# Top-k attention and a PReLU MLP on one core: small values of VectorE in a PSUM bank, the hidden layer in halves, MLP steps of two blocks side by side

## The chip, the core and the metric

The kernel runs on one core of a Trainium2 chip. The metric is the device time of one execution in microseconds (us); the time of a kernel is the median of several runs. Five engines work side by side, each with its own queue in program order: TensorE (PE, with its weight loads PEld), VectorE (DVE), ScalarE (ACT), GpSimd (POOL) and SyncE (SP), which here issues all DMAs. An instruction waits at the head of its engine's queue until what it needs is there.

## The reference

```python
def _attn_ref(q, k, v):            # (8, 8, 576, 64) each
    top_k = 32
    scale = 1.0 / np.sqrt(D)
    scores = scale * np.matmul(q, k.transpose(0, 1, 3, 2))
    kth = np.partition(scores, -top_k, axis=-1)[..., -top_k:-top_k + 1]
    scores = np.where(scores >= kth, scores, -1000000000.0)
    scores = scores - np.max(scores, axis=-1, keepdims=True)
    attn = np.exp(scores)
    attn = attn / (np.sum(attn, axis=-1, keepdims=True) + 1e-09)
    return np.matmul(attn, v)

def _moe_ref(x, w_in, w_out, alpha):   # x (4608, 512), d_ff 2048
    h = x @ w_in
    g = np.maximum(h, 0.0) + alpha * np.minimum(h, 0.0)
    return g @ w_out
```

Each of 64 heads has 576 x 576 scores; of each row only the 32 largest stay. The eight heads of a batch entry side by side are x, which goes through an MLP with a PReLU of one slope per hidden unit.

## The kernel before

A batch entry is a block: 576 tokens, eight heads in four pairs. The rows of scores are cut into duos of two tiles of 128 rows x 576; a pair has four duos of both heads' 128 rows, and two pairs share a fifth for their last 64 rows. So a block has 18 duos and the program 144. The last block takes its duos in the order of the tokens rather than of the pairs.

One turn of the main loop (lines 452 to 489) is a slot. It runs ten stages, each on another duo, so that a duo passes through the engines over several slots. `Ordered` (line 21) keeps every engine's instructions in the order in which the program is written, so the order of the calls in the loop is the order of the queues.

- `st_qk(n+2)` (line 150): TensorE computes the scores of the duo two ahead into `ps_sc`, four banks of PSUM with no second buffer. `st_exit(n+1)`: ScalarE copies scores to `s_sb`.
- `st_phase1(n)` (line 174), VectorE: MAX8 over six groups of 96 columns gives 48 candidates for each row, `cand`. `top` and `bot` (lines 185 and 186) are the elementwise larger and smaller of each second group and its neighbour in reverse; from these, with `hi`, `neg` and `n8`, comes a threshold near the 32nd largest, `p9[:, :, 0]`.
- `st_count(n-1)`, ScalarE: the sign against that threshold (`sg`) with its sum, `cs`, which is the count. `st_y(n-1)`, GpSimd: `y` = scores times `sg`.
- `st_phase2(n-2)` (line 216), VectorE: the eight largest of `y`; `eq` compares the constants `io9` with the count, `pk` picks with it from `p9`, a sum gives `KT`, the exact threshold.
- `st_relu(n-2)` (ScalarE), `st_sub(n-2)` (GpSimd) and `st_exp(n-3)` (ScalarE) mask the scores and take exp; SP's DMA transposes the weights to `wT`.
- `st_av(n-5)`: TensorE multiplies with v, with a column of ones for the sum (`xo`, or `xm` for the shared duo). `st_norm(n-5)` (line 271), VectorE: reciprocal `rz` and product, into `x`. `st_xT` (line 288): when a pair is through, SP's DMA transposes `x` into `xT`; with the fourth pair of a block, `mlp_ready` (line 311) queues the MLP of the block.
- `prep(n, 4)` (line 432): when a pair comes up in four slots, TensorE transposes its k and q (`tps`), ScalarE copies kT and VectorE qT.

The MLP of a block is a list of units (lines 309 to 361). Sixteen units compute 128 hidden rows each for all 576 tokens: eight matmuls into `ph`, in two halves of 288 columns in two banks, and one relu over both, in turn by VectorE and ScalarE (`relu`, line 365). The PReLU is split: w_out scaled by 1 - alpha takes the relu, and a product `w_lin_b` = w_in diag(alpha) w_out, computed once, takes x itself. Then each of five token tiles has two units that add both products into `pz`, 20 matmuls of 512 columns, and an output copy `o_sb`. At the end of each slot `owed` grows by 2.2 (4.0 in the last slots, up to 6.0) and units run while it is positive; a unit costs 1.0 to 2.6. There is one list, so a block's second product follows its first.

PSUM has eight banks: four for `ps_sc`, two for `ps_h` (`ph` and the transposes `tps`, one buffer of two banks), one for `pz`, one for `xo`.

The first slots also load the weights: two units a slot of `wt_units` (line 373), w_in first, then w_out, whose copies ScalarE scales.

If a threshold could not be found, a flag starts the general path behind the fast one; here it does not run.

Of the kernel before, what the change touches and what calls it, by code (L numbers as in the profile page):

```python
# [12 lines left out]
ALU = mybir.AluOpType  # L13
# [22 lines left out]
def fast_path(tc, q, k, v, moe_w_in, moe_w_out, moe_alpha, out, flag):  # L36
# [32 lines left out]
    with ExitStack() as ctx:  # L69
# [4 lines left out]
        qk_p = pool("qk", 5)  # L74
        s_p = pool("s", 6)
# [3 lines left out]
        xp = pool("xp", 2)  # L79
        ps_s = pool("ps_s", 1, space=PSUM)  # L80
        ps_h = pool("ps_h", 1, space=PSUM)
# [5 lines left out]
        io9 = const.tile([128, 9], FP32, name="io9")  # L87
# [10 lines left out]
        xs = [const.tile([128, 5, 128], BF16, name=f"x_{i}") for i in range(5)]  # L98
# [26 lines left out]
        def transpose_one(p, which, eng):  # L125
            t = st.pop((which, p))
            ps = ps_h.tile([128, 2, 512], FP32, name="tps", tag="h")
            for c in range(4):
                PE.transpose(ps[:, 0, 128 * c:128 * c + 128], t[:, c, :], ident_f)
            PE.transpose(ps[:, 1, 0:64], t[0:64, 4, :], ident_f[0:64, 0:64])  # L130
            dst = qk_p.tile([128, S], FP32, name=f"{which}T", tag=f"{which}T")
            if eng is ACT:
                ACT.copy(dst[:, 0:512], ps[:, 0, :])
                ACT.copy(dst[:, 512:S], ps[:, 1, 0:64])
            else:
                DVE.tensor_copy(dst[:, 0:512], ps[:, 0, :])
                DVE.tensor_copy(dst[:, 512:S], ps[:, 1, 0:64])
            (qT if which == "q" else kT)[p] = dst
# [35 lines left out]
        def st_phase1(n):  # L174
            s = T["s", n]
            c = two.tile([128, 2, NG, 8], FP32, name="cand", tag="cand")
# [7 lines left out]
            top = two.tile([128, 2, NG // 2, 8], FP32, name="top", tag="top")  # L184
# [3 lines left out]
            hi = two.tile([128, 2, 8], FP32, name="hi", tag="hi")  # L188
            for i in range(2):
                DVE.max(out=hi[:, i, :], in_=bot[:, i, :, :])  # L190
            DVE.tensor_scalar(neg[:, :, 0:24], top.rearrange("p a b c -> p a (b c)"), -1.0, None, ALU.mult)
            DVE.tensor_scalar(neg[:, :, 24:31], hi[:, :, 0:7], -1.0, None, ALU.mult)
            n8 = two.tile([128, 2, 8], FP32, name="n8", tag="n8")
# [6 lines left out]
        def st_count(n):  # L200
            s, p9 = T["s", n], T["p9", n]
            sg = two.tile([128, 2, S], BF16, name="sg", tag="sg")
# [13 lines left out]
        def st_phase2(n):  # L216
# [3 lines left out]
            eq = two.tile([128, 2, 9], FP32, name="eq", tag="eq")  # L220
# [6 lines left out]
        def st_relu(n):  # L227
            s = T["s", n]
            r = two.tile([128, 2, S], BF16, name="r", tag="r")
# [41 lines left out]
        def st_norm(n):  # L271
# [5 lines left out]
            if d[0] == "n":  # L277
                _, p, j = d
                DVE.tensor_tensor(xs[p % 5][:, j, :].rearrange("p (h d) -> p h d", h=2), xo[:, :, 0:64],
                                  rz[:, 0:2].unsqueeze(2).to_broadcast([128, 2, 64]), ALU.mult)  # L280
            else:
                for i in range(2):
                    DVE.tensor_tensor(xs[d[1 + i] % 5][0:64, 4, :].rearrange("p (h d) -> p h d", h=2),
# [4 lines left out]
        def st_xT(n):  # L288
# [3 lines left out]
            for p in ps_:  # L292
# [7 lines left out]
                if b < B - 1:  # L300
                    SP.dma_start_transpose(t, xs[p % 5].rearrange("p a b -> p (a b)"))
                else:
                    SP.dma_start_transpose(t[:, j:j + 1, :], xs[p % 5][:, j, :])
# [5 lines left out]
        units = []  # L309

        def mlp_ready(b, j):
# [6 lines left out]
            gt = gp.tile([128, NFT, ntok], BF16, name="gT", tag="gT")  # L318
            if ntok == S:
                def unit(f):  # L320
                    ph = ps_h.tile([128, 2, 512], FP32, name="ph", tag="h")
                    for hh in range(2):
                        for kk in range(4):
                            PE.matmul(ph[:, hh, 0:288], w_in_b[kk][:, 128 * f:128 * f + 128],
# [127 lines left out]
        for n in range(ND + 9):  # L452
# [9 lines left out]
            if on(n - 1):  # L462
                st_y(n - 1)
# [316 lines left out]
```

## Time and profile before

| | us |
|---|---|
| median of 3 runs | 1562.38 |
| lowest and highest | 1562.21, 1563.31 |
| profiled execution | 1564.27 |
| its span in the profile | 1562.4 |
| VectorE busy | 1204.5 (77%) |
| TensorE busy | 976.3 (62%) |
| ScalarE busy | 835.7 (53%) |
| GpSimd busy | 765.1 (49%) |
| mean granted TensorE clock | 0.69 of full |

The profile names buffers without their numbers, so `p` is p9, `n` is n8, `io` is io9 and `x` and `w` are the tiles of x and of the attention weights. A busy TensorE is not TensorE at its peak. All helper calls have line 31, so rows are told apart by tiles. The number in square brackets at the end of a row of the time order is the idle time ahead of it and what ended it.

### The profile page before, as it was taken

To read this page: it belongs to the slowest core of one execution; us is meant where nothing else is said; L and a number is where in the kernel's file an instruction comes from. 1 tells how busy PE (TensorE), PEld (TensorE's weight loads), DVE (VectorE), ACT (ScalarE), POOL (GpSimd) and SP (SyncE) were. 2 spreads that over 40 slices of the span, in tenths; PEclk is the share of its full clock that TensorE was granted. 3 is DMA by queue.
4 is the path that set the end of the run, shared out by engine and by line. 5 is a ranking of instruction groups with operands and counts; after the bars stand their busy time and mean duration, and the time that the engine had idled before them with its cause. 6 is when DMAs were issued, how large, how long until landed. Compare 5 with 4: busy or idle time off the path is not lost.

```text
span 1562.4 us, 18744 instructions
## 1 busy us (share of the span) xinstructions
PE 976.3 (62%) x5248; PEld 533.3 (34%) x5282; DVE 1204.5 (77%) x4191; ACT 835.7 (53%) x1360; POOL 765.1 (49%) x676
## 2 busy tenths in 40 slices
PE   4432365776567774777657675567647746468776
PEld 2221133443234332443334333343324423234444
DVE  5985545799948998599957999499976975948891
ACT  3564644566626665366635666266644654535561
POOL 4653443466525655256625666156643553514550
PEclk9755575578655885568756886578855777657878
DMA  3534422234321343124312343214331243202222
GB/s 89 120 101 101 102 46 57 49 64 94 69 37 40 84 79 68 41 45 101 70 37 48 79 88 60 48 34 86 76 65 41 57 91 72 46 18 45 61 53 49
DMA packets 346000, 102.00 MB, mean 65 GB/s; under 512 B 337168, under 2 KB 337184, under 8 KB 345888
## 3 DMA queue, kind: packets, MB, share of 16 engines
q1 hardware_dynamic: 345888, 100.73, 30.4%
q8 instruction: 44, 0.72, 0.2%
q14 instruction: 68, 0.56, 0.1%
HBM read 36.71 MB, written 9.44 MB: 30 GB/s over the span
## 4 chain that ended last, share of the span: by engine, by line
DVE 62%; PE 19%; ACT 8%; DMA 4%; issue 3%; SPq 2%; POOL 1%; ACTq 0%; POOLq 0%; DVEq 0%
DVE cand L31 14%; DVE p L31 12%; PE ph L31 11%; DVE bot L31 8%; DVE pk L31 6%; PE ps_sc L31 4%; DVE neg L31 3%; DVE top L31 3%; DVE eq L31 3%; ACT sg L31 3%; DVE gT L31 3%; SPq L31 2%; DVE n L31 2%; DVE x L31 2%; PE tps L31 2%
## 5 line engine op out<-in xcount | busy, mean ns | idle before, releaser
L31 POOL TENSOR_TENSOR y<-s_sb,sg 128x576 f32<-128x576 f32 x288 | 362.2, 1279 | 620.2 <-ACT sg L31 620.2
L31 PE MATMUL ps_sc<-kT,qT 64*128 64x64 f32 (+3 forms) x1280 | 308.7, 624 | 241.6 <-ACT s_sb L31 240.5
L31 POOL TENSOR_TENSOR s_sb<-s_sb,r 128x576 f32<-128x576 f32 x288 | 363.5, 1283 | 119.9 <-ACT r L31 119.6
L31 PE MATMUL ph<-xT,w_in_b 128*128 128x288 bf16 (+2 forms) x1216 | 240.6, 367 | 132.0 <-DMA xT<-x 45.9
L31 ACT ACTIVATE sg<-s_sb,p 128x576 bf16<-128x576 f32 x288 | 220.3, 767 | 138.2 <-DVE rz L31 130.7
L31 DVE MAX8 cand<-s_sb 128x8 f32<-128x96 f32 x1728 | 288.9, 244 | 3.5 <-ACT s_sb L31 3.5
L31 PEld LDWEIGHTS ps_sc<-kT,qT 64*128 64x128 f32 (+1 forms) x1280 | 147.3, 253 | 394.8 <-ACT s_sb L31 254.5
L31 ACT ACTIVATE r<-s_sb,KT 128x576 bf16<-128x576 f32 x288 | 207.5, 768 | 115.4 <-DVE KT L31 113.3
L31 DVE MAX8 p<-y 128x8 f32<-128x576 f32 x288 | 204.0, 747 | 31.3 <-POOL y L31 31.3
L31 PEld LDWEIGHTS <-w_in_b 128*128 128x128 bf16 x1216 | 138.4, 129 | 220.6 <-issue 145.5
L31 DVE TENSOR_SCALAR gT<-ph 128x576 bf16<-128x576 f32 (+2 forms) x66 | 48.7, 738 | 181.9 <-PE ph L31 181.9
L31 ACT ACTIVATE gT<-ph 128x576 bf16<-128x576 f32 (+2 forms) x66 | 41.9, 635 | 273.3 <-PE ph L31 273.1
L31 PEld LDWEIGHTS <-wT 128*128 128x128 bf16 (+3 forms) x1600 | 109.0, 112 | 214.0 <-issue 146.9
L31 PE MATMUL xo<-v,wT 128*128 128x65 bf16 (+1 forms) x1280 | 114.6, 214 | 102.4 <-DVE x L31 78.6
L31 ACT ACTIVATE w<-s_sb 128x1152 bf16<-128x1152 f32 x144 | 165.4, 1149 | 0.0
L31 PE MATMUL pz<-w_out_b,gT 128*128 128x512 bf16 (+1 forms) x638 | 165.0, 406 | 0.2 <-issue 0.2
L31 ACT COPY s_sb<-ps_sc 128x1152 f32<-128x1152 f32 x144 | 158.2, 1098 | 7.4 <-PE ps_sc L31 7.4
L31 DVE TENSOR_TENSOR bot<-cand 128x48 f32<-128x48 f32 x144 | 159.8, 1109 | 0.0
L31 DVE SCALAR_TENSOR_TENSOR pk<-eq,p 128x18 f32<-128x18 f32 x144 | 108.9, 756 | 5.0
L31 PEld LDWEIGHTS <-gT 128*128 128x128 bf16 (+1 forms) x640 | 66.9, 109 | 83.5 <-issue 26.9
L31 DVE TENSOR_TENSOR top<-cand 128x48 f32<-128x48 f32 x144 | 70.8, 492 | 4.9
L31 DVE COPY qT<-tps 128x512 f32<-128x512 f32 x64 | 26.1, 449 | 62.1 <-PE tps L31 62.1
(48 smaller groups left out, 799.4 us busy)
## 6 DMA issues: line engine op xcount, KB each, us to landing
k_st<-in_k_dram SPq DMA_DIRECT2D x64, 128.0 KB, 2.6
q_st<-in_q_dram SPq DMA_DIRECT2D x64, 128.0 KB, 2.5
v_st<-in_v_dram SPq DMA_DIRECT2D x64, 128.0 KB, 2.4
out_dram<-o_sb SPq DMA_DIRECT2D x32, 256.0 KB, 2.5
w_st<-in_moe_w_in_dram SPq DMA_DIRECT2D x16, 256.0 KB, 3.5
w_st<-in_moe_w_out_dram SPq DMA_DIRECT2D x16, 256.0 KB, 3.3
wT<-w SPq DMA_TRANSPOSE x144, 3.4
k_st<-in_k_dram SPq DMA_DIRECT2D x64, 16.0 KB, 2.2
```

The lines of the kernel that those rows point to most:

```text
L31: return self.tc.keep_in_program_order(f(*a, **kw))
```

## The change

- A PSUM bank of its own, `small` (pool `ps_d`), holds values that VectorE alone uses: the constants `io9`, every second group of candidates (`lo`), `top`, `hi`, `n8` and `eq`, in two places that duos take in turn. The other groups of candidates (`up`), `bot`, `neg`, `p9` and `pk` stay in SBUF. `bot` is computed ahead of `top`.
- That bank comes from `ps_h`, which has one now. `ph` is one half of 288 columns, a step is four matmuls and a relu of 288; 32 steps make a block. The transposes of k and q go through the one bank in two pieces, 512 columns and the 64-column tail (`tpt`), each with its copy.
- The MLP has two lists, `fq` for the first product and `oq` for the second, whose units are quarters of a token tile: one matmul with `w_lin_b` and four with `w_out_b`. A block's second product is queued when its first is through, and the next block's first product may run beside it. At a block's first step all second-product units of the block two before are run.
- In a slot there are three places for a first-product step and two for a second-product one, fed by allowances of 1.9 and 1.2 a slot (at most 6.0 and 4.0), and of 4.5 and 2.5 from slot 130 on, with three more of each at the end of such slots. `st_xT` moves behind the scores of the slot.
- Buffers: qT and kT 4 each instead of 5, `s_sb` 5 instead of 6, `x` 4 instead of 5, `xT` 3 instead of 2; `sg` and `r` share three where they had two each. `gT` of the last block has its own tag. The loop is one turn shorter.

```diff
-        qk_p = pool("qk", 5)
-        s_p = pool("s", 6)
+        qk_p = pool("qk", 4)
+        s_p = pool("s", 5)
...
+        small = ps_d.tile([128, 512], FP32, name="small")
+        io9 = small[:, 500:509]
...
-            ps = ps_h.tile([128, 2, 512], FP32, name="tps", tag="h")
+            ps = ps_h.tile([128, 512], FP32, name="tps", tag="h")
             for c in range(4):
...
+            copy(dst[:, 0:512], ps)
+            ps = ps_h.tile([128, 64], FP32, name="tpt", tag="h")
+            PE.transpose(ps, t[0:64, 4, :], ident_f[0:64, 0:64])
+            copy(dst[:, 512:S], ps)
...
-                    DVE.max(out=c[:, i, g, :], in_=s[:, i, GW * g:GW * g + GW])
-            up, lo = c[:, :, 0::2, :], c[:, :, 1::2, ::-1]
+                    DVE.max(out=(lo if g % 2 else up)[:, i, g // 2, :], in_=s[:, i, GW * g:GW * g + GW])
...
-            DVE.tensor_tensor(top, up, lo, ALU.max)
-            DVE.tensor_tensor(bot, up, lo, ALU.min)
+            DVE.tensor_tensor(bot, up, lo[:, :, :, ::-1], ALU.min)
+            DVE.tensor_tensor(top, up, lo[:, :, :, ::-1], ALU.max)
...
-            eq = two.tile([128, 2, 9], FP32, name="eq", tag="eq")
+            eq = small[:, 240 * (n % 2) + 128:240 * (n % 2) + 146].rearrange("p (i c) -> p i c", i=2)
...
+            r = two.tile([128, 2, S], BF16, name="r", tag="sg", bufs=3)
...
+            def unit(i):
+                if i == 0:
+
+                    while oq and oq[0][0] <= me - 2:
+                        oq.pop(0)[1]()
...
+                    f, t0 = i // 2, 288 * (i % 2)
+                    for kk in range(4):
+                        PE.matmul(ph, w_in_b[kk][:, 128 * f:128 * f + 128],
+                                  flat[kk][:, t0:t0 + 288], start=(kk == 0), stop=(kk == 3))
+                    relu(gt[:, f, t0:t0 + 288], ph)
...
+                PE.matmul(z[0:m, :], flat[a][:, t0:t0 + m], w_lin_b[a], start=(a == 0), stop=False)
+                for f in range(4 * a, 4 * a + 4):
...
-        for n in range(ND + 9):
+        for n in range(ND + 8):
...
+            end = n >= ND - 14
+            fo = min(fo + (4.5 if end else 1.9), 6.0)
+            oo = min(oo + (2.5 if end else 1.2), 4.0)
...
                 st_y(n - 1)
+            f_unit()
             if on(n):
                 st_phase1(n)
...
                 st_norm(n - 5)
-                st_xT(n - 5)
+            f_unit()
+            o_unit()
             if on(n + 2):
                 st_qk(n + 2)
+            f_unit()
+            o_unit()
+            if on(n - 5):
+                st_xT(n - 5)
             prep(n, 4)
...
+            if end:
+                for _ in range(3):
+                    f_unit()
+                    o_unit()
```

Three places show how the order of the engines changes. The first is VectorE in phase 1, with the waits on semaphores in brackets (DVE_49 is VectorE's own). Before, from the last candidates to the threshold p:

```order
L31 MAX cand<-s_sb 128x8 x11
L31 TENSOR_TENSOR top<-cand 128x48 [waits DVE_49]
L31 TENSOR_TENSOR bot<-cand 128x48
L31 MAX hi<-bot 128x8 [waits DVE_49]
L31 MAX hi<-bot 128x8
L31 TENSOR_SCALAR neg<-top 128x2x24
L31 TENSOR_SCALAR neg<-hi 128x2x7 [waits DVE_49]
L31 MAX n_10947<-neg 128x8 [waits DVE_49]
L31 MAX n_10947<-neg 128x8
L31 TENSOR_SCALAR p_10950<-n_10947 128x2 [waits DVE_49]
```

After, `small` standing for lo, top, hi and n8:

```order
L31 MAX small<-s_sb 128x8 [waits DVE_49]
L31 TENSOR_TENSOR bot<-up,small 128x48 [waits DVE_49]
L31 TENSOR_TENSOR small<-up,small 128x48
L31 MAX small<-bot 128x8 [waits DVE_49] x2
L31 TENSOR_SCALAR neg<-small 128x2x24 [waits DVE_49]
L31 TENSOR_SCALAR neg<-small 128x2x7
L31 MAX small<-neg 128x8 [waits DVE_49] x2
L31 TENSOR_SCALAR p_7165<-small 128x2 [waits DVE_49]
```

The same instructions, with bot ahead of top, and with more of them waiting for VectorE's own semaphore; five of the six MAX into `small` ahead of bot have such a wait too.

The second is VectorE where a block ends, from the product of the shared duo (xm) to the candidates of the next slot. Before:

```order
L31 TENSOR_TENSOR x_132<-xm,rz 64x128
L31 TENSOR_TENSOR x_133<-xm,rz 64x128
L31 TENSOR_SCALAR gT<-ph 128x576 x3
L31 MAX p_5521<-y 128x8 x2
L31 TENSOR_TENSOR eq<-io_103,cs 128x18
L31 SCALAR_TENSOR_TENSOR pk<-eq,p_5521 128x18
L31 TENSOR_REDUCE KT<-pk 128x2
L31 MAX cand<-s_sb 128x8 x12
```

After:

```order
L31 TENSOR_TENSOR x_137<-xm,rz 64x128
L31 TENSOR_TENSOR x_138<-xm,rz 64x128
L31 MAX p_6993<-y 128x8 x2
L31 TENSOR_TENSOR small<-small,cs 128x18
L31 SCALAR_TENSOR_TENSOR pk<-small,p_6993 128x18
L31 TENSOR_REDUCE KT<-pk 128x2
L31 TENSOR_SCALAR gT<-ph 128x288
L31 MAX up<-s_sb 128x8
```

Three relus of 576 columns stood behind x; now one of 288 stands between KT and the candidates.

The third is TensorE where a pair's k and q are transposed, from the end of the attention product. Before:

```order
L31 MATMUL xo<-v_3_117,wT 128x65
L31 MATMUL ps_sc<-kT,qT 128x512 x2
L31 MATMUL ps_sc<-kT,qT 128x64 x2
L31 MATMUL tps<-ident_f,k_st 128x128 x4
L31 MATMUL tps<-ident_f,k_st 128x64
L31 MATMUL tps<-ident_f,q_st 128x128 x4
L31 MATMUL tps<-ident_f,q_st 128x64
```

After, from the last matmul of a quarter of the second product (pz) that stands behind a half of ph:

```order
L31 MATMUL pz<-w_out_b_150,gT 128x512
L31 MATMUL ps_sc<-kT,qT 128x512 x2
L31 MATMUL ps_sc<-kT,qT 128x64 x2
L31 MATMUL tps<-ident_f,k_st 128x128 x4
L31 MATMUL tpt<-ident_f,k_st 128x64
L31 MATMUL tps<-ident_f,q_st 128x128 x4
L31 MATMUL tpt<-ident_f,q_st 128x64
```

MLP steps now stand between the attention product and the scores, and each tail is a tile of its own in the one bank.

## Rows read from the trace of the kernel before

**Rows 1.** The page, part 1: busy time, share of the span and instructions.
```profile
PE 976.3 (62%) x5248; PEld 533.3 (34%) x5282; DVE 1204.5 (77%) x4191; ACT 835.7 (53%) x1360; POOL 765.1 (49%) x676
```

**Rows 2.** Windows: length; busy (instructions) PE, PEld, DVE, ACT, POOL; PEclk, DMA, GB/s.
```profile
838.80:974.30 135.50, 89.50 (x504) 47.68 (x505) 131.33 (x459) 88.19 (x143) 83.83 (x72) 0.76 0.35 70
797.20:838.80 41.60, 26.89 (x116) 15.07 (x117) 16.58 (x51) 10.73 (x19) 7.55 (x6) 0.52 0.22 46
1344.00:1523.00 179.00, 122.05 (x733) 71.03 (x735) 143.69 (x471) 93.09 (x150) 82.99 (x66) 0.68 0.21 44
1523.00:1562.30 39.30, 27.25 (x269) 17.48 (x269) 5.87 (x18) 7.83 (x12) 2.52 (x2) 0.89 0.22 50
```

**Rows 3.** VectorE in order of time, one slot: start us, length us, operation.
```profile
709.41 0.17 DVE L31 TENSOR_REDUCE KT<-pk 128x2 f32<-128x18 f32 x1
709.50 2.01 DVE L31 MAX8 cand<-s_sb 128x8 f32<-128x96 f32 x12
711.54 0.33 DVE L31 TENSOR_TENSOR top<-cand 128x48 f32<-128x48 f32 x1
711.80 1.31 DVE L31 TENSOR_TENSOR bot<-cand 128x48 f32<-128x48 f32 x1
...
715.79 0.70 DVE L31 TENSOR_TENSOR eq<-io,cs 128x18 f32<-128x18 f32 x1
716.53 1.20 DVE L31 SCALAR_TENSOR_TENSOR pk<-eq,p 128x18 f32<-128x18 f32 x1
717.76 0.17 DVE L31 TENSOR_REDUCE KT<-pk 128x2 f32<-128x18 f32 x1
```

**Rows 4.** Instructions by tile: ns shortest/median/longest, first and last start us, shapes.
```profile
L31 DVE TENSOR_TENSOR bot<-cand x144: 193/1309/1319, 14.9 to 1511.0; 128x48 f32<-128x48 f32 x144
L31 DVE SCALAR_TENSOR_TENSOR pk<-eq,p x144: 177/1177/1208, 29.1 to 1521.5; 128x18 f32<-128x18 f32 x144
L31 DVE TENSOR_TENSOR x<-xo,rz x128: 290/291/293, 60.8 to 1527.0; 128x128 bf16<-128x128 f32 x128
L31 DVE RECIPROCAL rz<-xo x128: 155/163/172, 60.6 to 1526.7; 128x2 f32<-128x2 f32 x128
L31 POOL TENSOR_TENSOR s_sb<-s_sb,r x288: 1268/1279/1340, 31.4 to 1525.1; 128x576 f32<-128x576 f32 x144
```

**Rows 5.** VectorE and TensorE in order of time, at the start of two blocks.
```profile
623.19 0.76 DVE L31 TENSOR_SCALAR gT<-ph 128x576 bf16<-128x576 f32 x1 [5.16 <-PE ph L31]
...
802.61 1.36 PE L31 MATMUL ph<-xT,w_in_b 128*128 128x288 bf16 x5 [0.93 <-DMA xT<-x]
...
804.01 0.76 DVE L31 TENSOR_SCALAR gT<-ph 128x576 bf16<-128x576 f32 x1 [5.17 <-PE ph L31]
```

**Rows 6.** TensorE and VectorE in order of time, where a pair is transposed.
```profile
867.73 1.41 PE L31 MATMUL tps<-ident_f,q_st 128*128 128x128 f32 x5 [1.66 <-ACT kT L31]
...
869.45 0.81 DVE L31 COPY qT<-tps 128x512 f32<-128x512 f32 x2
```

**Rows 7.** TensorE in order of time: scores, attention product and pz at both clock levels.
```profile
854.93 2.40 PE L31 MATMUL ps_sc<-kT,qT 64*128 64x512 f32 x8 [1.48 <-ACT s_sb L31]
...
863.50 1.30 PE L31 MATMUL ps_sc<-kT,qT 64*128 64x512 f32 x8 [1.46 <-ACT s_sb L31]
...
884.61 0.81 PE L31 MATMUL pz<-w_lin_b,xT 128*128 128x512 bf16 x3 [0.16 <-issue]
...
887.08 0.78 PE L31 MATMUL xo<-v,wT 128*128 128x65 bf16 x10
...
900.39 1.49 PE L31 MATMUL pz<-w_lin_b,xT 128*128 128x512 bf16 x3 [0.34 <-issue]
```

**Rows 8.** VectorE in order of time: the KT reductions that end two stages.
```profile
232.36 0.17 DVE L31 TENSOR_REDUCE KT<-pk 128x2 f32<-128x18 f32 x1
...
1343.95 0.17 DVE L31 TENSOR_REDUCE KT<-pk 128x2 f32<-128x18 f32 x1
```

**Rows 9.** Waits of ScalarE from 110 to 235 us: total us, times, longest us.
```profile
ACT w_out_b L31 <- DMA w_st<-in_moe_w_out_dram: 45.7, 11, 7.5
```

More of the change, by code (lines that the diff above doesn't have):

```diff
@@ L78, in fast_path @@
         gp = pool("gp", 2)
-        xp = pool("xp", 2)
+        xp = pool("xp", 3)
         ps_s = pool("ps_s", 1, space=PSUM)
+        ps_d = pool("ps_d", 1, space=PSUM)
         ps_h = pool("ps_h", 1, space=PSUM)
@@ L97, in fast_path @@
             POOL.memset(t[:, :, S:640], 0.0)
-        xs = [const.tile([128, 5, 128], BF16, name=f"x_{i}") for i in range(5)]
+        xs = [const.tile([128, 5, 128], BF16, name=f"x_{i}") for i in range(4)]
         for t in xs:
@@ L201, in st_count @@
             s, p9 = T["s", n], T["p9", n]
-            sg = two.tile([128, 2, S], BF16, name="sg", tag="sg")
+            sg = two.tile([128, 2, S], BF16, name="sg", tag="sg", bufs=3)
             cs = three.tile([128, 2], FP32, name="cs", tag="cs", bufs=4)
@@ L342, in mlp_ready @@
[L342 to L361 removed]
+            me = len(made)
@@ new lines, in mlp_ready @@
+            made.append(0)
+            hold = {}
+            big = ntok == S
+            cw = 288 if big else 4 * ntok
+            def unit(i):
+                if i == 0:
+                    while oq and oq[0][0] <= me - 2:
+                        oq.pop(0)[1]()
+                    hold["g"] = gp.tile([128, NFT, ntok], BF16, name="gT", tag="gT" if big else "gs")
+                gt = hold["g"]
+                ph = ps_h.tile([128, cw], FP32, name="ph", tag="h")
+                if big:
+                    f, t0 = i // 2, 288 * (i % 2)
[3 more added lines that the diff above has]
+                    relu(gt[:, f, t0:t0 + 288], ph)
+                else:
+                    for e in range(4):
+                        f = 4 * i + e
+                        for kk in range(4):
+                            PE.matmul(ph[:, ntok * e:ntok * e + ntok], w_in_b[kk][:, 128 * f:128 * f + 128],
+                                      flat[kk][:, tok0:tok0 + ntok], start=(kk == 0), stop=(kk == 3))
+                    relu(gt[:, 4 * i:4 * i + 4, :].rearrange("p a t -> p (a t)"), ph)
+                if i == nu - 1:
+                    for t0 in range(tok0, tok0 + ntok, 128):
+                        for a in range(4):
+                            oq.append((me, lambda t0=t0, a=a: part(t0, a)))
@@ new lines, in mlp_ready, with part @@
+            nu = 32 if big else 4
+            for i in range(nu):
+                fq.append((me, lambda i=i: unit(i)))
+            def part(t0, a):
+                m = min(128, tok0 + ntok - t0)
+                gt = hold["g"]
+                if a == 0:
+                    hold["z"] = ps_z.tile([128, DMODEL], FP32, name="pz", tag="z")
+                z = hold["z"]
+                PE.matmul(z[0:m, :], flat[a][:, t0:t0 + m], w_lin_b[a], start=(a == 0), stop=False)
+                for f in range(4 * a, 4 * a + 4):
+                    PE.matmul(z[0:m, :], gt[:, f, t0 - tok0:t0 - tok0 + m], w_out_b[f],
+                              start=False, stop=(f == NFT - 1))
+                if a == 3:
+                    o = io.tile([128, DMODEL], FP32, name="o_sb", tag="io")
+                    ACT.copy(o[0:m, :], z[0:m, :])
+                    SP.dma_start(out[S * b + t0:S * b + t0 + m, :], o[0:m, :])
```

101 lines of the change are left out of this document (31 added, 70 removed).

## Prediction

> **What bounds the kernel now.** I read the page's busy shares first [rows 1]: VectorE is busy 77% of the 1562.4 us span and no other engine over 62%, but a share over the whole span mixes stages. The windows [rows 2] separate them. From 838.80 to 974.30, 16 slots (a slot is one turn of the main loop, from one KT reduction to the next), VectorE is busy 131.33 of 135.50 us: it sets the pace, at 8.47 us a slot, of which ScalarE needs 5.5 and GpSimd 5.2. From 797.20 to 838.80, two slots, it is busy 16.58 of 41.60: there it waits. One slot of the first kind in order of time [rows 3] is without gaps, yet three instructions on 18 to 48 numbers per partition take 0.70, 1.20 and 1.31 us.
>
> The instructions by tile [rows 4] say why. bot runs from 193 to 1319 ns and pk from 177 to 1208 at one and the same shape; seven forms do this (eq, top, the two neg and p<-n are the others), and all of them take their inputs from SBUF. Instructions with one operand in PSUM do not vary: x takes 290 to 293 ns over 128 instances, rz 155 to 172. The ceiling of the spread is one GpSimd instruction, 1279 ns in the median (the last row of the group). So these small instructions stand behind GpSimd's tensor_tensor of the moment, and a PSUM operand spares x that.
>
> **Part 1, small values to PSUM.** With eq, pk, bot and top at their shortest (0.16, 0.18, 0.19, 0.21 us), the slot of [rows 3], 8.35 us from KT to KT, becomes 8.35 - 0.54 - 1.02 - 1.12 - 0.12 = 5.55 us.
>
> Added: waits of VectorE on itself. The order shows that `small` is guarded as one thing: the second MAX into hi, the second into n8 and the first neg now wait for the instruction ahead. In [rows 3] cand, which waits for nothing on VectorE, starts 0.08 us before KT ends, and KT, which waits for pk, 0.03 us after pk ends, so a wait costs 0.11 us. Three are 0.33; neg<-hi loses one, mostly covered, and I take 0.30. The five waits between the MAX into `small` reach back over an `up` MAX, whose pitch of 0.16 us (twelve in 2.01) covers them: 0, or 5 x 0.11 = 0.55 us a slot if the `up` counts too. No row of before has VectorE write to PSUM; between a gain, which nothing excludes, and some dearer write I take zero, by rz and x, which read PSUM at no visible surcharge.
>
> [...]
>
> **Part 2, h in halves and overlapped blocks.** The work keeps its size. A block of 18 slots has 32 halves, 1.78 a slot, and 20 quarter parts of five matmuls, 1.11 a slot. Half of the relus fall to VectorE: a 576-column relu takes 0.76 us [rows 5], 288 columns then some 0.45, and 0.37 with the overlap to the next: 0.89 x 0.37 = 0.33 us a slot. The two qT copies (0.81 us together [rows 6]) come four times in 18 slots and get one more wait: 0.19. The slot becomes 5.55 + 0.30 + 0.33 + 0.19 = 6.37 us; ScalarE and GpSimd come close but stay under it. 18 slots are 114.7 us; today a block is 804.01 - 623.19 = 180.8 us [rows 5].
>
> At a block's start three relus in a row each wait 5 us for two steps of eight matmuls, and the next slot waits too. The new code spends at most three halves a slot, so this burst goes. What is late next there is the transpose of x: VectorE goes idle at 798.84 (804.01 less 5.17), and ph goes on at 802.61 [rows 5], 3.8 us later. The first half's relu now stands between phase 2 (1.8 us) and phase 1, so VectorE waits 3.8 + 0.6 + 0.1 - 1.8 = 2.7 us, once a block.
>
> The remaining edits I cost at nothing. With five s buffers the copy of slot n+1 takes the one that exp read a slot earlier on the same engine. In the ring of three for sg and r, r waits for the y of its slot before, which phase 2 has waited for anyway, and sg for a subtraction that exp has waited for. Four buffers of qT and kT hold at most three pairs until the last block, four of x those of two pairs and the next two. The transposes of x on SP now stand behind the store of an output tile, which waits for ScalarE's o_sb: up to 1 us in the 2.7, once a block, if a store falls there; wT, behind them in SP's queue, is wanted two slots later.
>
> **Where time comes back.** The q and k transposes stay behind the scores on TensorE and gain two round trips, since the 64-column tails now wait for the head's copy out of the one bank. In [rows 6] the q transposes end at 869.14 and VectorE takes up the copy at 869.45: just in time at 8.4 us a slot. VectorE will be there 2 us sooner, and the two tails add some 0.8 us. So 2.8 us of waiting, four times a block: 11.2 us. Bounds: 0 if TensorE gets to it sooner, 5 us each if a quarter part stands in front.
>
> [...] By [rows 7] a matmul of 512 columns has a pitch of 0.43 or 0.216 us (three in 1.49 and 0.81 us, less the last one's 0.634 or 0.379, over two). A slot's scores are 2.40 or 1.30, xo 0.78 or a little more, the halves 1.78 x 0.96 or 0.49, the parts 1.11 x 2.14 or 1.08, the transposes 0.22 x 2.82 or half: 7.9 us at the lower level, 4.5 at the higher. At 6.37 us the lower one does not fit in the 11 slots of a block that hold both kinds of MLP work: 11 x 1.5 = 17 us if all were slow, 0 if none. I take a third, 5.5 us, since the steady stretch, with the same round trips, has the higher level half of its time.
>
> A block is then 114.7 + 2.7 + 11.2 + 5.5 = 134.1 us.
>
> **The sum**, along the KT marks of [rows 8].
> To 232.36 us: nine slots of today, from 30 us on, are VectorE's and lose 2 us each; the others wait for weights behind SP's queue (ScalarE for w_st, 45.7 us [rows 9]) and keep their time. 232.4 - 18 = 214.4.
> 232.36 to 1343.95: 1111.6 us, six blocks of 180.8 and 26.8 us where the loads of the last block's four pairs come close together on SP; their order is the same, I keep 26. 6 x 134.1 + 26 = 830.6.
> From there to the end, 218.4 us today. VectorE is busy 143.69 of the first 179.00 us and TensorE 122.05 [rows 2]. VectorE sheds 46, but TensorE inherits the twenty parts that the sixth of the eight blocks leaves behind, 20 x 1.08 = 22 us: 144 us of TensorE, some 17 of waits, and the same tail of 39: 200.
> 214.4 + 830.6 + 200 = 1245 us of span. The profiled execution took 1564.27 us against its span of 1562.4; the median of the runs is 1562.38. With 1.9 us on top: 1247 us.
>
> **The rivals.**
> TensorE becomes the bound. Halves, parts and transposes that share one bank keep it waiting for relus, the clock stays low, and slots stay at 8.35 us: a block 18 x 8.35 + 2.7 = 153; 6 x 153 + 26 + 214 + 205 + 2 = 1365. For it: 7.9 us of slow work, and 0.52 granted where TensorE was busy 26.89 of 41.60. Against: 0.76 at the same share in the steady stretch.
> Operands in PSUM cost more than rz shows. x takes 98 ns more than the shortest bot for 80 columns more; 0.03 us each at most, 0.2 a slot, 30 us: 1277. [...]
> The contention stays, because a PSUM operand does not spare these forms. Slots are 8.65 us, and only the boundary's 28 us go: a block 180.8 - 28 + 8 = 161; 6 x 161 + 26 + 232 + 212 + 2 = 1438. Against: x and rz.
> No stall comes back, all is VectorE's: 6 x 114.7 + 26 + 212 + 185 + 2 = 1113.
> Slower: the one ps_h bank. Every half waits for the relu of the half ahead, which stands in VectorE's queue behind phase 1 or in ScalarE's behind exp; the scores, placed behind the second half, are late, and then the copy of the scores, the count and y. It decides from 10.05 - 6.37 = 3.7 us of waiting in every slot; two waits of 2.1 us make 10.6 us a slot and a block 194: 6 x 194 + 26 + 232 + 215 + 2 = 1639. Against: ScalarE has 3 us of each 8.47 to spare.
>
> **How the numbers follow.** Forecast 1247 (1150 to 1310 with its bounds) 0.54, TensorE-bound 0.17, PSUM surcharge 0.08, contention stays 0.08, no stall 0.08, slower 0.04, no effect 0.01. From 1150 to 1400 lie the first three, 0.79. A measurement of this kernel can tell about 0.2% from no change. Faster 0.95, same 0.01, slower 0.04.
>
> **What would show it.** Right: bot, pk, eq, top, neg and p<-n constant at 160 to 230 ns; 5.9 to 6.5 us from KT to KT in a plain slot; no run of ph steps at a block's start; VectorE idle before qT in four slots of 18. Wrong: a spread up to 1.3 us that stays; VectorE idle before gT in most slots, with a clock near 0.5; a pitch of 0.27 us between the MAX into `small`; a last stretch that is longer than today's.

## The result, and the profile after

The changed kernel takes 1296.82 us in the median (1288.59 to 1304.06, four runs) beside 1562.75 for the kernel before (four runs): a ratio of 0.8297, 95% interval 0.8247 to 0.8347. It is faster, as forecast, and inside the range; the point, 1247, was 50 us too low. The profiled execution took 1296.23 us, of which the span is 1294.2.

Busy time, share of the span and instructions, part 1 of the page of after (compare [rows 1]):

```profile
PE 881.2 (68%) x5282; PEld 481.4 (37%) x5282; DVE 896.7 (69%) x4247; ACT 836.6 (65%) x1416; POOL 759.8 (59%) x675
```

VectorE lost 307.8 us of busy time at a few more instructions. Over the whole span no engine stands out any more: four lie between 59 and 69%. That share mixes stages. In the six blocks, in the windows below, VectorE is busy 670.94 of 846.50 us, more than any other engine, and of the 136.0 us of a block (the mean of five) it waits 18.3.

VectorE of after by tile: ns shortest/median/longest, first and last start, shapes (compare [rows 4]):

```profile
L31 DVE TENSOR_TENSOR bot<-up,small x144: 203/204/206, 14.5 to 1229.9; 128x48 f32<-128x48 f32 x144
L31 DVE SCALAR_TENSOR_TENSOR pk<-small,p x144: 176/176/179, 28.7 to 1240.0; 128x18 f32<-128x18 f32 x144
L31 DVE TENSOR_TENSOR small<-small,cs x144: 156/165/167, 28.5 to 1239.8; 128x18 f32<-128x18 f32 x144
L31 DVE MAX8 small<-bot x288: 194/195/196, 14.9 to 1230.4; 128x8 f32<-128x24 f32 x144
```

bot, whose median was 1309 ns, is constant at 204, and pk at 176 in place of 1177. One slot of VectorE in order of time, start and length in us (compare [rows 3]):

```profile
561.13 0.17 DVE L31 TENSOR_REDUCE KT<-pk 128x2 f32<-128x18 f32 x1
561.22 0.25 DVE L31 MAX8 up<-s_sb 128x8 f32<-128x96 f32 x1
...
563.27 0.20 DVE L31 TENSOR_TENSOR bot<-up,small 128x48 f32<-128x48 f32 x1
...
565.36 0.45 DVE L31 TENSOR_SCALAR gT<-ph 128x288 bf16<-128x288 f32 x1
...
567.05 0.17 DVE L31 TENSOR_TENSOR small<-small,cs 128x18 f32<-128x18 f32 x1
567.25 0.18 DVE L31 SCALAR_TENSOR_TENSOR pk<-small,p 128x18 f32<-128x18 f32 x1
567.46 0.17 DVE L31 TENSOR_REDUCE KT<-pk 128x2 f32<-128x18 f32 x1
```

The slot is 6.33 us from KT to KT with a relu in it and 5.96 to 5.97 without; it was 8.35. The stretches of after by windows (length; busy of PE, PEld, DVE, ACT, POOL; granted clock), cut at the KT marks that answer to [rows 8]:

```profile
28.90:219.10 190.20, 85.51 (x411) 44.48 (x412) 105.78 (x508) 112.20 (x182) 98.48 (x92) 0.64 0.41 95
219.10:1065.60 846.50, 619.51 (x3727) 336.31 (x3725) 670.94 (x3184) 610.63 (x1044) 564.28 (x489) 0.82 0.41 82
1065.60:1240.20 174.60, 130.23 (x876) 72.72 (x873) 103.53 (x478) 97.48 (x165) 82.58 (x67) 0.89 0.25 53
1240.20:1294.20 54.00, 30.61 (x219) 19.34 (x219) 5.32 (x18) 6.78 (x10) 3.82 (x4) 0.63 0.15 32
```

The six blocks went from 1111.6 to 846.5 us and the start from 232.4 to 219.1; the end went from 218.4 to 228.6, so it grew by 10 us. All of the gain is in the blocks and the start.

VectorE and TensorE in order of time at a block's start and in the slot behind it, where a pair is transposed; in brackets the idle time and what ended it (compare [rows 5, 6]):

```profile
511.10 0.40 PE L31 MATMUL ph<-xT,w_in_b 128*128 128x288 bf16 x1 [4.39 <-DMA xT<-x]
...
512.87 0.46 DVE L31 TENSOR_SCALAR gT<-ph 128x288 bf16<-128x288 f32 x1 [2.67 <-PE ph L31]
...
518.77 0.65 PE L31 MATMUL tps<-ident_f,k_st 128*128 128x128 f32 x4 [0.55 <-DVE gT L31]
520.10 0.27 PE L31 MATMUL tpt<-ident_f,k_st 64*128 64x64 f32 x1 [0.68 <-ACT kT L31]
520.67 0.66 PE L31 MATMUL tps<-ident_f,q_st 128*128 128x128 f32 x4 [0.30 <-ACT kT L31]
...
521.37 0.69 DVE L31 COPY qT<-tps 128x512 f32<-128x512 f32 x1 [2.65 <-PE tps L31]
522.42 0.22 DVE L31 COPY qT<-tpt 128x64 f32<-128x64 f32 x1 [0.36 <-PE tpt L31]
```

The burst of three relus is gone. What is left are one wait for xT, behind it one or two shorter waits for the next halves (1.0 to 3.2 us a block), and, four times a block, the chain of k and q through the one bank. VectorE's largest waits over the whole span (total us, times, longest):

```profile
DVE qT L31 <- PE tps L31: 117.2, 32, 16.7
DVE gT L31 <- PE ph L31: 110.8, 44, 20.7
DVE p L31 <- POOL y L31: 44.2, 20, 7.8
```

### The profile page after: what moved, and what is told of

The parts are those of the page before. It is cut to its first block, busy times and chain, and to the rows that moved or that the text cites. A ratio compares the mean times of both kernels' runs of the same rounds, so it can differ in the third digit from the quotient of the medians.

```text
span 1294.2 us, 18779 instructions
## 1 busy us (share of the span) xinstructions
PE 881.2 (68%) x5282; PEld 481.4 (37%) x5282; DVE 896.7 (69%) x4247; ACT 836.6 (65%) x1416; POOL 759.8 (59%) x675
## 4 chain that ended last, share of the span: by engine, by line
DVE 46%; PE 24%; ACT 13%; DMA 6%; issue 4%; SPq 3%; POOL 3%; ACTq 0%; POOLq 0%
DVE small L31 15%; DVE p L31 11%; DVE up L31 6%; PE pz L31 6%; PE ph L31 6%; PE ps_sc L31 4%; PE tps L31 4%; SPq L31 3%; ACT sg L31 3%; DVE gT L31 3%; DMA w_st<-in_moe_w_out_dram 2%; ACT r L31 2%; DVE neg L31 2%; ACT s_sb L31 2%; DVE x L31 2%
## 5 line engine op out<-in xcount | busy, mean ns | idle before, releaser
L31 POOL TENSOR_TENSOR y<-s_sb,sg 128x576 f32<-128x576 f32 x288 | 361.8, 1277 | 409.6 <-ACT sg L31 409.6
L31 PE MATMUL ps_sc<-kT,qT 64*128 64x64 f32 (+3 forms) x1280 | 256.3, 533 | 102.4 <-ACT s_sb L31 102.3
L31 PE MATMUL ph<-xT,w_in_b 128*128 128x288 bf16 (+2 forms) x1216 | 212.7, 316 | 162.6 <-DVE gT L31 63.2
L31 DVE MAX8 p<-y 128x8 f32<-128x576 f32 x288 | 204.2, 747 | 44.2 <-POOL y L31 44.2
L31 ACT ACTIVATE r<-s_sb,KT 128x576 bf16<-128x576 f32 x288 | 207.2, 768 | 33.7 <-DVE KT L31 27.5
L31 PEld LDWEIGHTS ps_sc<-kT,qT 64*128 64x128 f32 (+1 forms) x1280 | 126.1, 216 | 268.9 <-issue 148.2
L31 DVE MAX8 small<-s_sb 128x8 f32<-128x96 f32 x864 | 216.7, 251 | 0.0
L31 DVE MAX8 up<-s_sb 128x8 f32<-128x96 f32 x864 | 211.1, 244 | 3.1 <-ACT s_sb L31 3.1
L31 PEld LDWEIGHTS <-w_in_b 128*128 128x128 bf16 x1216 | 114.8, 111 | 201.8 <-issue 164.9
L31 PE MATMUL pz<-w_out_b,gT 128*128 128x512 bf16 (+1 forms) x640 | 187.0, 420 | 0.0
L31 PE MATMUL xo<-v,wT 128*128 128x65 bf16 (+1 forms) x1280 | 113.1, 212 | 49.0 <-DMA wT<-w 28.2
L31 DVE TENSOR_SCALAR gT<-ph 128x288 bf16<-128x288 f32 (+2 forms) x122 | 56.7, 465 | 110.9 <-PE ph L31 110.8
L31 ACT ACTIVATE gT<-ph 128x288 bf16<-128x288 f32 (+2 forms) x122 | 50.8, 416 | 120.3 <-PE ph L31 120.3
L31 PE MATMUL pz<-w_lin_b,xT 128*128 128x512 bf16 (+1 forms) x160 | 70.6, 441 | 2.8 <-ACT o_sb L31 2.7
```

Of the source, the lines that this page charges most:

```text
L31: return self.tc.keep_in_program_order(f(*a, **kw))
```

## The experiments

The theory was that the two parts take away two separate things, the contention of small SBUF operands with GpSimd and the burst of first-product steps at a block's start, and that the transposes give some of it back. The rival was that one of the parts does all of it, or that small instructions are slow for a reason other than GpSimd. A question came with the result: where the 50 us beyond the forecast lie. Lengths of the stretches of every run, from the KT marks of its profile (us; a block is the mean of the five that hold no stall of loads):

| kernel | time | start | one block | six blocks | end |
|---|---|---|---|---|---|
| before | 1562.8 | 232.4 | 181.2 | 1111.6 | 218.4 |
| after | 1296.8 | 219.1 | 136.0 | 846.5 | 228.6 |
| e1_sbuf | 1495.2 | 233.3 | 164.3 | 1010.9 | 248.1 |
| e2_onelist | 1469.4 | 218.4 | 166.8 | 1039.4 | 207.1 |
| e3_qact | 1288.4 | 220.5 | 134.5 | 837.2 | 228.6 |
| e4_spread | 1285.9 | 219.7 | 136.8 | 850.6 | 216.6 |
| e5_tails | 1260.9 | 215.7 | 131.2 | 813.5 | 230.6 |
| e6_late | 1301.2 | 216.6 | 138.4 | 859.6 | 222.9 |
| e7_nosub | 1424.0 | 219.4 | 164.4 | 1011.9 | 191.0 |
| e8_all | 1251.5 | 214.2 | 132.4 | 822.7 | 212.1 |
| e9_split | 1308.4 | 217.0 | 137.7 | 857.5 | 229.0 |
| e10_three | 1264.9 | 216.7 | 133.2 | 828.1 | 218.1 |
| e11_even | 1254.2 | 215.6 | 133.3 | 828.5 | 203.6 |
| e12_best | 1231.3 | 214.7 | 130.4 | 809.7 | 205.5 |

**e1_sbuf: only the place of the small values undone.**

```
-        small = ps_d.tile([128, 512], FP32, name="small")
+        small = const.tile([128, 512], FP32, name="small")
```

> The changed kernel with the one tile small in SBUF instead of in its PSUM bank; order, waits and everything else as they are. Theory (a PSUM operand spares these instructions the turn of GpSimd's tensor_tensor): bot, pk, eq, top, neg and p spread again from 0.2 to 1.3 us, some 2.4 us a slot come back, plain slots are 8.3 to 8.7 us, VectorE busy near 1230 us, the time 1440 to 1560 us (part of it is absorbed by the waits for qT and gT that the changed kernel has). Rival (the order of bot and top, the own-semaphore waits and the new MLP schedule made the gain, the place does not matter): 1285 to 1310 us and constant durations.

Measured: 1495.2 us, 0.9574 of before (0.9560 to 0.9588). Same order, same waits, another memory, and the spread is back:

```profile
L31 DVE TENSOR_TENSOR bot<-up,small x144: 207/333/1280, 14.5 to 1429.5; 128x48 f32<-128x48 f32 x144
L31 DVE SCALAR_TENSOR_TENSOR pk<-small,p x144: 178/1197/1204, 29.0 to 1438.9; 128x18 f32<-128x18 f32 x144
```

So the memory in which the operands lie is the cause, not the rewriting of the chain.

**e2_onelist: the small values stay in PSUM, but the MLP steps run from one list at a slot's end, as before.**

```
-            fo = min(fo + (4.5 if end else 1.9), 6.0)
-            oo = min(oo + (2.5 if end else 1.2), 4.0)
+            owed = min(owed + (4.0 if end else 2.2), 6.0)
...
+            while (fq or oq) and owed > 0:
```

> The changed kernel with the MLP in one list as before: halves and quarter parts, each block's second product right behind its first, run at the slot's end by one allowance of 2.2 a slot (4.0 in the last 14, at most 6.0), a half at 0.5 and a part at 1.1, and the transpose of x ahead of the scores. Theory (the overlap of two blocks takes away the burst at a block's start and nothing else): plain slots stay at 6.0 to 6.3 us, each block begins with some twelve halves at 1.8 us and the wait for xT, 20 to 30 us more per block at the start; the time 1380 to 1480 us. Rival (once VectorE is fast, TensorE's sum of work sets the time whatever the order): within 20 us of 1297.

Measured: 1469.4 us, 0.9408 (0.9394 to 0.9422). Plain slots are 5.97 us, but the slots at a block's start 27.5 and 19.7 us, and VectorE waits for the first product 117 times:

```profile
DVE gT L31 <- PE ph L31: 286.2, 117, 5.7
```

With before, e1, e2 and after, the parts stand nearly in a square: the values without the schedule give 92 us, the schedule without the values 66, both 266. The square is not clean, since e1 and e2 both keep the halves, the one bank for the transposes and the other numbers of buffers. The two parts are not separate. A slot lasts as long as its slower side: with the burst left in, TensorE's steps between two relus hold up two slots and faster VectorE instructions only wait longer; with the contention left in, VectorE holds 8.2 to 8.5 us in a plain slot and the MLP steps hide behind that.

**e7_nosub: the kernel before without the masking subtraction on GpSimd** (the weights are the exponentials of all scores).

```
-                POOL.tensor_tensor(s[:, i, :], s[:, i, :], r[:, i, :], ALU.subtract)
+                pass
```

> The kernel before with one part left out: the masking subtraction on GpSimd, half of GpSimd's large instructions; the weights are then the exponentials of all scores. Theory (VectorE's small instructions stand behind the GpSimd instruction of the moment): bot, pk, eq and top keep their longest of some 1.2 to 1.3 us, but about half as often, their sum over a slot falls from 2.8 us above the shortest to 1 to 1.8 us, and the time falls to 1340 to 1460 us. Rival (they are slow for a reason of their own, in SBUF, whatever GpSimd does): the mean of bot and pk as before, 1540 to 1565 us.

Measured: 1424.0 us in a single run, inside the theory's range. The small values lie in SBUF as before, and only GpSimd does less:

```profile
L31 DVE TENSOR_TENSOR bot<-cand x144: 193/202/1320, 14.9 to 1376.3; 128x48 f32<-128x48 f32 x144
L31 DVE SCALAR_TENSOR_TENSOR pk<-eq,p x144: 177/179/1204, 29.1 to 1384.3; 128x18 f32<-128x18 f32 x144
```

The longest stay as they were, and fewer are caught: 118 of 144 bot and 82 of 144 pk last over 0.5 us before, 46 and 51 here, about half of them together, as the theory had it. The medians fall to the shortest because less than half are left; the means are 513 and 530 ns where they were 1109 and 756. The trace of the kernel before shows what they stand behind. GpSimd in the slot of [rows 3]:

```profile
710.54 2.51 POOL L31 TENSOR_TENSOR s_sb<-s_sb,r 128x576 f32<-128x576 f32 x2 [1.19 <-ACT r L31]
...
715.19 2.51 POOL L31 TENSOR_TENSOR y<-s_sb,sg 128x576 f32<-128x576 f32 x2 [2.14 <-ACT sg L31]
```

GpSimd's second instruction of each pair ends at 713.05 and 717.70 us; bot ends at 713.11 and pk at 717.73. Over the whole run the long bot and pk end 0.06 and 0.03 us, in the median, after a GpSimd instruction. So it is GpSimd's instruction of the moment that the small ones stand behind. For bot and pk that is up to 1.1 us on an instruction of 0.2.

**e3_qact: the q copies on ScalarE.**

```
-                    transpose_one(p, "q", DVE)
+                    transpose_one(p, "q", ACT)
```

> The changed kernel with the copies of the q transposes on ScalarE, as those of k, instead of on VectorE. Theory (VectorE's 131 us of waits for qT, four slots of 10 us in 18, are the chain of k transposes, copies, q transposes in one bank, and cost time because VectorE stands in that chain): those waits go, the four slots fall to 6.3 to 8 us, ScalarE takes some 25 us of copies; 1210 to 1255 us. Rival (ScalarE, with 5.5 to 6 us a slot, is the next bound: the count behind the copies is late, y is late and VectorE waits for GpSimd's y instead): 1280 to 1310 us, with VectorE's wait for y well over its 44 us.

Measured: 1288.4 us, 0.8261 (0.8232 to 0.8289). The theory missed: the 8 us below the changed kernel are inside the spread of the two kernels' runs. VectorE's waits for q are gone, but most of the same time stands elsewhere:

```profile
DVE gT L31 <- PE ph L31: 199.0, 74, 20.7
DVE p L31 <- POOL y L31: 66.4, 31, 10.3
DVE rz L31 <- PE xo L31: 50.1, 18, 12.2
```

The time is in the rival's range, and VectorE does wait longer for y, 66.4 us where it was 44.2. But more of it stands before the first product, 199.0 where it was 110.8. TensorE waits 44.0 us before the tails where it waited 47.6: the chain through the bank is about as long whoever copies, and the next half waits behind it.

**e5_tails: the 64-column tails through the bank of xo.**

```
-            ps = ps_h.tile([128, 64], FP32, name="tpt", tag="h")
+            ps = ps_x.tile([128, 64], FP32, name="tpt", tag="x")
```

> The changed kernel with one edit: the 64-column tails of the k and q transposes go through the bank of xo instead of the one bank of h, so that a tail need not wait for the copy of its head. Theory (the round trips that the single bank of h adds to the transposes are a term of their own): TensorE waits 47.6 us in all before the tails, 32 pairs of them; 20 to 45 us come off the 1296.8, so 1252 to 1277 us, and the slots that hold transposes go from some 10.3 to 9.2 us. Rival (the heads and the scores ahead of them set the chain, and the tails now wait for xo): 1288 to 1305 us, the same slots at 10 us or more.

Measured: 1260.9 us, 0.8065 (0.8045 to 0.8085): 36 us less than the changed kernel, all of it in the start and the blocks. The slots with transposes fall from 10.3 to 9.2 us and below. Here the chain itself became shorter: TensorE no longer waits 47.6 us in all for the copy ahead of a tail, and VectorE has no wait of its own for it (compare 520.10 and 522.42 us in after):

```profile
575.17 0.27 PE L31 MATMUL tpt<-ident_f,k_st 64*128 64x64 f32 x1
...
576.50 0.27 PE L31 MATMUL tpt<-ident_f,q_st 64*128 64x64 f32 x1
576.61 0.69 DVE L31 COPY qT<-tps 128x512 f32<-128x512 f32 x1 [2.08 <-PE tps L31]
577.22 0.21 DVE L31 COPY qT<-tpt 128x64 f32<-128x64 f32 x1
```

**e6_late: a new block's first half one place later.**

```
+            new = {len(made) - 1} if n > 5 and made and mark[0] != len(made) else set()
+            mark[0] = len(made)
...
-                if fq and fo >= 1:
+                if fq and fo >= 1 and not (first and fq[0][0] in new):
...
-            f_unit()
+            f_unit(True)
```

> The changed kernel with one edit: where a block has become ready in the slot before, the first half of its first product is not placed at the head of the next slot but at the second place, behind the products with v. Theory (VectorE waits 2.7 us once a block because the transpose of x on the DMA queue has not landed): seven waits of 2.7 us go, and 10 to 19 us come off the 1296.8, so 1278 to 1287 us, with no wait of TensorE for xT over 1 us in the six middle blocks. Rival (the half is late anyway, and the same wait falls on the next slot): 1293 to 1300 us.

Measured: 1301.2 us, 0.8340 (0.8324 to 0.8355). The theory missed, and it was the wait that I had forecast most closely. TensorE's waits for xT fall from 50.3 to 36.4 us over the span, not to nothing. The slot of the wait gets shorter by 1.4 us in the mean of the six blocks: VectorE no longer waits for the first half there, but waits 5.6 to 6.9 us for q where it waited 2.7 to 3.1. The slot behind the transposes then lasts 7.6 to 9.9 us where it was 6.33. In one block, in order of time:

```profile
660.65 0.69 DVE L31 COPY qT<-tps 128x512 f32<-128x512 f32 x1 [5.61 <-PE tps L31]
...
664.18 1.12 PE L31 MATMUL ph<-xT,w_in_b 128*128 128x288 bf16 x4 [0.88 <-DVE gT L31]
...
667.36 3.35 PE L31 MATMUL ps_sc<-kT,qT 64*64 64x512 f32 x16
670.64 0.66 PE L31 MATMUL ph<-xT,w_in_b 128*128 128x288 bf16 x4
...
671.34 0.46 DVE L31 TENSOR_SCALAR gT<-ph 128x288 bf16<-128x288 f32 x1 [3.08 <-PE ph L31]
```

TensorE has a half and a part in front of the scores of a slot of 64-row tails, which are sixteen matmuls and run partly at the lower level (3.35 us at a granted clock of 0.64; 2.18 us at 0.98 in the rows of e9 below); VectorE waits 3.08 us for what stands behind. TensorE was short of time in these slots with or without the wait for xT, so moving the wait gained nothing.

**e9_split: q one slot behind k.**

```
+            if owing:
+                transpose_one(owing.pop(0), "q", DVE)
...
+                    if 0 < p < KPB * (B - 1):
+                        owing.append(p)
+                    else:
+                        transpose_one(p, "q", DVE)
```

> The changed kernel with one edit: in the seven blocks ahead of the last one the q transposes of a pair stand one slot behind its k transposes (both were in one slot). Theory (VectorE waits for q because the k transposes and ScalarE's copy of them stand ahead in the one bank of h): 27 waits of some 2.5 us for the head of q shrink to 0.5 to 1 us, and the slots of 10.3 us to 7.5 to 8; some of it goes to the k slot: 20 to 55 us come off, 1242 to 1277 us. Rival (the transposes delay the next half and the next copy of the scores wherever they stand): 1285 to 1305 us.

Measured: 1308.4 us, 0.8385 (0.8371 to 0.8399), 12 us more than the changed kernel and above the theory's and the rival's range. Some slots gain as expected (8.56 in place of 10.4), but the first pair of a block meets the sixteen-matmul scores again:

```profile
668.03 2.18 PE L31 MATMUL ps_sc<-kT,qT 64*64 64x512 f32 x16
...
671.73 0.60 PE L31 MATMUL tps<-ident_f,q_st 128*128 128x128 f32 x4
...
672.37 0.69 DVE L31 COPY qT<-tps 128x512 f32<-128x512 f32 x1 [5.90 <-PE tps L31]
```

**e4_spread: the second product of the last full block, the seventh, forced out at the second token group of the last block, not forced until the third.** (The code counts from 0, so later expectations call this block the sixth.)

```
-                    while oq and oq[0][0] <= me - 2:
+                    while oq and oq[0][0] <= me - 2 and (big or me >= B + 1):
```

> The changed kernel with one rule altered: the second-product units of the last full block are no longer run all at once before the second token group of the last block (17 quarter parts in a row, a slot of 30.9 us with VectorE waiting 20.7 us for gT), but spread by the allowance, at the latest before the third group four slots later. Theory (the run in one place blocks the attention's TensorE work and so VectorE): that slot falls to some 12 us, the next ones grow by 2 to 3 us each, the time falls by 5 to 20 us. Rival (TensorE sets the time of the whole last stretch, where a piece of work stands does not matter): within 5 us of 1297.

Measured: 1285.9 us, 0.8237 (0.8222 to 0.8251); the end falls by 12 us. In the changed kernel VectorE stands still here while TensorE clears fifteen quarter parts, from 1166.32 us on (the expectation had seventeen):

```profile
1166.32 0.39 PE L31 MATMUL pz<-w_lin_b,xT 128*128 128x512 bf16 x1
...
1184.15 1.03 PE L31 MATMUL pz<-w_out_b,gT 128*64 128x512 bf16 x4
1185.11 1.07 PE L31 MATMUL ph<-xT,w_in_b 128*128 128x128 bf16 x16
...
1186.22 0.69 DVE L31 TENSOR_SCALAR gT<-ph 128x512 bf16<-128x512 f32 x1 [20.68 <-PE ph L31]
```

**e8_all: e4, e5 and e6 together.** 

> The changed kernel with three edits: tails of the transposes through the bank of xo, the first half of a new block one place later, and the second product of the sixth block not forced out until the third token group of the last block. If the three costs are separate (theory), the time is 1297 less some 11 for the last, 10 to 19 for the middle one and 20 to 45 for the first: 1222 to 1256 us. Rival (they share one chain on TensorE, and what one gives the next wait takes): 1262 to 1285 us.

Measured: 1251.5 us, 0.8016 (0.8002 to 0.8029). It is in the theory's range, but not by the theory's sum: the gains of e4 and e5 alone make 1250, which leaves nothing for e6 here either.

**e10_three (e4, e5 and e9 together) and e11_even (the same with evener allowances at the end).**

```
-            fo = min(fo + (4.5 if end else 1.9), 6.0)
-            oo = min(oo + (2.5 if end else 1.2), 4.0)
+            fo = min(fo + (3.0 if end else 1.9), 6.0)
+            oo = min(oo + (1.8 if end else 1.2), 4.0)
```

> The changed kernel with three edits: tails of the transposes through the bank of xo, q one slot behind k in the first seven blocks, and the second product of the sixth block not forced out until the third token group. If the three add up, 1297 less 36, less what the split alone gives, less 11: 1195 to 1230 us. If tails and split take the same wait, 1235 to 1252 us.

> The kernel of the three edits with one more: the allowances of the last 14 slots at 3.0 halves and 1.8 quarter parts a slot instead of 4.5 and 2.5. Theory (the last stretch pays for a burst: TensorE crowded in the first eight slots, idle in the later ones): 6 to 20 us less than with three edits, and slots of 7 to 8.5 us in place of 9 to 11 at the start of the stretch. Rival (what is not done there has to be done behind the last slot, where nothing covers it): the same time within 4 us, or more.

Measured: 1264.9 us (0.8099, 0.8085 to 0.8112), more than either expectation: the split spoils here too. And 1254.2 us (0.8040, 0.8024 to 0.8055): the evener allowances give 10.7 us, and the end falls from 218.1 to 203.6, 6.6 us of it up to the last KT and 8.0 behind it. Seven slots there are 6.3 to 7.9 us where a burst of halves had made them 8 to 11; a later slot, where the third token group forces out what is left, now takes 28.2 us. TensorE was not idle in the later slots of the changed kernel, as the theory had it: from 1192.1 to 1210.0 us, at 5.96 us a slot, it is busy 17.06 of 17.90 us.

**e12_best: e5, e4 and the evener allowances.** 

> The changed kernel with the three edits that have helped by themselves: tails of the transposes through the bank of xo (-36 us), the second product of the sixth block not forced out until the third token group (-11), and the evener allowances of the last 14 slots (-11). If they add up, 1297 less 58: 1239 us, and 1232 to 1246 is taken as adding up. Rival: the last two edits are about one stretch and share a gain: 1247 to 1255 us.

Measured: 1231.3 us (1230.0 to 1232.5, five runs), 0.7881 of before (0.7870 to 0.7892): 65.5 us less than the changed kernel, more than the 58 of the single edits and just past the 1232 to 1246 that were to count as adding up, and the fastest of all. Its blocks and the two parts of its end:

```profile
214.70:1024.30 809.60, 599.43 (x3681) 330.77 (x3716) 668.99 (x3184) 606.91 (x1044) 564.62 (x489) 0.83 0.44 86
1024.30:1177.70 153.40, 119.75 (x858) 67.62 (x867) 103.42 (x478) 95.11 (x163) 82.71 (x67) 0.94 0.27 57
1177.70:1229.90 52.20, 32.62 (x236) 19.70 (x238) 5.33 (x18) 7.94 (x13) 3.86 (x4) 0.74 0.19 43
```

VectorE's waits for the first product from 1024 to 1178 us (total, times, longest):

```profile
DVE gT L31 <- PE ph L31: 44.0, 14, 19.8
```

The longest, 19.8 us, is a run of forced parts again, now ahead of the third token group: the end is evener, but not even.

## Why the prediction was right, and where it was off

**The contention**: right, in kind and size. The forecast slot was 5.55 + 0.30 = 5.85 us without a relu, and 0.37 more with one; measured 5.97 and 6.33. In the mean, with relus and qT copies, it was 6.37; VectorE's own time in a block, its waits taken off, is 117.7 us, 6.54 a slot. e1 and e7 show the cause from both sides.

**The PSUM surcharge**: the forecast took zero, and the trace of after shows a little on some forms and nothing on others. bot's 204 ns stand against a shortest of 193 in SBUF, pk's 176 against 177; the second MAX form came to 195, against 178 in the median for the same form in SBUF; the most is 207 in the mean for the neg of 48 columns, against a median of 170. The rival that gave 1277 took 0.2 us a slot. The plain slot is 0.12 us over its forecast, about 17 us over 144 slots, so 0.12 of that rival's 0.2 us at most came true.

**The waits of VectorE on itself**: the three of 0.11 us were not measured apart; between the MAX into `small` there is none. In the slot above the twelve MAX take 2.05 us from the first start to bot's, against 2.04 in [rows 3] from cand's start to top's; the five waits cost nothing.

**The wait for xT**: forecast 2.7 us, measured 2.67 in the block shown and 2.63 to 2.67 in four of five. As a price of its own it was still wrong: e6 moved it and no time came back, since TensorE was late behind it; VectorE's waits for q grew from 12.4 to 16.3 us a block.

**The transposes**: 2.8 us of waiting, four times a block, 11.2 in all. Measured 2.65 + 0.36 in the slot shown, from 1.7 to 3.7 in others, and 12.4 a block. e3 shows that the chain is what costs, e5 what the tails' two round trips are worth, 36 us in all.

**The block**: forecast 134.1, measured 133.8 to 138.2, mean 136.0; the stall of loads 26 forecast, 166.5 - 136.0 = 30.5 measured. Six blocks are 15.9 us over. That a block came within 2 us is partly luck. VectorE's own work was 3.0 us more than the 114.7 of the sum and the waits for q 1.2 more; against that stand 5.5 us for TensorE's clock, a third of its bound, where VectorE's other waits for the first product come to 2.3. The two levels that the trace of before shows at [rows 7] are granted clocks of 0.50 and 1.00, and my third was an estimate from the 0.76 granted from 838.80 to 974.30 us, the steady stretch [rows 2]; the windows of after grant 0.82 over the blocks. What the clock took by itself in the blocks no run shows.

**The start**: 4.7 us over. The nine slots and the stretch behind them shed 13.3 us, not 18.

**The end was the mis-sized term**: 228.6 us against 200, 28.6 of the 49 us that the span is over. The step was "144 us of TensorE, some 17 of waits, and the same tail of 39". TensorE's work was less than that, 130.2 us of the 174.6; the waits were 44.4, not 17, and the tail 54.0. I had priced the second product as work and given no thought to when it runs. The parts that the sixth block leaves behind are not what hurts: 17 of the twenty run singly, between the attention's steps, from 1066 to 1137 us. What runs in one piece are fifteen parts of the seventh block, forced out by the second token group, while VectorE waits 20.68 us; in the kernel before, that block's second product ran a unit at a time from 1427 to 1465 us. And the allowances of 4.5 and 2.5 crowd the first slots of the stretch, at 8 to 11 us. VectorE's waits for the first product in this stretch are 61.5 us, 31.3 before and 44.0 in e12. e4 took 12.0 us off the end and the evener allowances 14.5. With both the end is 205.5 us: most of the 28.6 us is the order of that work, not its amount. The tail is 14.7 us longer than before, and the trace shows from what. TensorE's waits for transposes in it (total, times, longest; the wait for wT begins 3.0 us ahead of the tail):

```profile
PE ph L31 <- DMA xT<-x: 8.8, 4, 2.6
PE xo L31 <- DMA wT<-w: 5.9, 1, 5.9
```

Neither stands in the tail of before, and TensorE is busy 30.6 us in this one against 27.3, at a granted clock of 0.63 against 0.89. What the clock is worth there, e11 and e12 show roughly: tails of 239 and 236 matmuls keep TensorE busy 28.6 us at 0.85 and 32.6 at 0.74.

**The rivals**: "TensorE becomes the bound" fell, as plain slots run at VectorE's pace; but it holds in single slots, behind a block's start and at the end, and at the end the forecast lost 28.6 of its 49 us. "The contention stays" fell with the constant bot and pk, "slower through one bank" with the waits: VectorE waits for the first product 44 times, not in every slot. "No stall" fell with the 18.3 us of waits in a block.

## What to carry to other kernels

Where small VectorE instructions vary by a factor of six at one shape, look at what GpSimd runs at that moment, and put an operand into PSUM before counting instructions. A wait is worth its length only if the engine that it hands the work to has room behind it: e3, e6 and e9 moved waits of 2 to 5 us and gave between 8 us, which is inside the spread of the runs, and a loss of 12, while e5, which shortened the chain, gained 36. Work that is put off must be priced with the place at which it then runs.

## What the runs showed of the hardware

The seven forms that vary have all their operands in SBUF. Whether a pk is caught goes by where it falls against GpSimd's instruction: in before all 82 that last over 0.5 us start while one runs, and none of the other 62 does. When caught, bot and pk end 0.06 and 0.03 us behind it, in the median. Not every form in SBUF is caught: in before hi took 165 to 189 ns and the sum into KT 171 to 174. Halving GpSimd's large instructions about halved what this costs: the seven forms that vary took 2.55 us a slot above their shortest before and 1.24 in e7. The medians of bot and pk hide it, since they went from 1309 and 1177 ns to 202 and 179, with the longest at 1320 and 1204: means or counts are to be compared. A change of order can switch which one is caught: in e1, with GpSimd's work whole and bot ahead of top, bot's mean was 510 ns and top's 1014, where they were 1109 and 492.
